# The last two token chunks of a fused attention and gated feed-forward kernel: first-layer blocks by seven half products, and a tail in a written step order

## The chip, the cores and the metric

The kernel runs on one core of a Trainium2 chip. A core has five engines with instruction queues of their own: TensorE (PE; its weight loads are shown as PEld), VectorE (DVE), ScalarE (ACT), GpSimd (POOL) and SyncE (SP, which here issues DMAs). Each takes its instructions in order, and semaphores tie them together. The metric is the device time of one execution in microseconds, the median of several runs.

## The reference, cut to what matters

The input is q, k and v of 8 batches, 8 heads, 576 positions and 64 values per head. Attention is computed twice, once on positions averaged by fours and once within a band of three neighbours, and the two are added. The result, 4608 tokens of 512 values, goes through a gated feed-forward layer:

```
x    = attention output, as (4608, 512)
gate = max(x @ w_gate, 0)        # w_gate 512 x 1536
val  = x @ w_val                 # w_val  512 x 1536
out  = (gate * val) @ w_out      # w_out 1536 x 512
```

The change is in this layer alone, in its last 1024 tokens.

## The kernel before, in words

Attention works on 32 head pairs. Its output lies transposed in xT: four blocks of 128 model values (index kk) by 4608 tokens, f16. The feed-forward layer works on nine chunks (0 to 8) of 512 tokens.

**First layer.** For a chunk c and a block jj of 128 of the 1536 ff values, `emit_h_mm` (line 585, its matmul at 588) makes the gate's half of the block by four matmuls (128x128 weights, 512 tokens, one for each kk) into one PSUM bank, and the value's half by four into the next. `emit_relu` (L605, ACT) writes max(gate, 0) as f16 into r1, and `emit_gate` (L609, DVE) multiplies r1 by the value's bank into gT[c % 2], block jj, f16. PSUM has eight banks of 512 f32 columns: `pair(i)` is banks 2i and 2i+1.

**Second layer.** A `Unit` (class at L655) makes 256 tokens (u = 0 or 1) of a chunk. It is already a two-by-two block product with seven products in place of eight: the 12 ff blocks are two halves of six, the 256 tokens two halves of 128, the 512 outputs two halves of 256. DVE forms four sums of gT blocks (s1 to s4, L678), the sums of w_out are made once (`emit_wt`, L651), and the steps p1 to p7 (`mm`, L684) are six matmuls of 256 columns each. Products p1, p6, p7 and p4 add up in one region a, and between them ACT copies a away (`keep`, L718) so that the partial sums can be used; p5 and p3 add up in b, p2 is alone in d. DVE adds d or b to a kept copy and writes the output tile (c11 at L721, c12 at L725, c22 at L733), ACT copies a itself (c21, L729). `emit_out` (L635) issues the output DMAs on SP.

**What sets the order.** The engines are scheduled by hand: instructions go into each queue in the order in which the Python code emits them. Chunks 2 to 6 follow a written order of steps, ORDER, in `emit_periods`; a step's mark `<` or `>` moves it to the chunk before or after. The last part, from the end of chunk 6's first layer, follows loops: `emit_tail_slot` for eight slots (chunks 7 and 8, three ff blocks each), each with half of the second-layer products of the chunk before, then the two units of chunk 8, `last`, one after the other in step order p1, p2, p6, p5, p7, p4, p3. In the first tail slot three gate matmuls and three value matmuls of chunk 7 are put ahead of product p2, into the banks of `pair(1)`.

The tail's units keep their sums in buffers that attention has left: `sa` in the tiles of v (shown as vw), `sums` in a q tile and two v tiles.

The softmax here doesn't subtract the row's maximum and nothing guards it: scores larger than these inputs give would overflow.

## Time and profile before

| | us |
|---|---|
| median of 8 runs | 350.72 |
| lowest and highest of them | 348.71, 351.86 |
| the profiled execution, its own time | 350.76 |
| its span, from first to last instruction | 348.9 |
| PE busy in the span | 340.2 |
| DVE, ACT, POOL busy | 274.8, 214.6, 190.7 |
| first product of unit (6,0), where the tail begins | 275.91 |
| start of the last DVE instruction | 345.69 |

Times within the span are counted from its start. A profile page has the busy time of each engine, the span in 40 slices of 8.7 us with a digit for the busy tenths of each, the DMA queues, the chain of work that ended last (followed back from the last instruction to whatever released each step), and the costliest groups of instructions. A group's line has the source line, the engine, the operation, the tiles written and read, shapes and count, then busy us and the mean ns of one, then the idle time ahead of them and who ended it. [...]

### The profile page before, as it was taken

To read this page: it belongs to the slowest core of one execution; us is meant where nothing else is said; L and a number is where in the kernel's file an instruction comes from. 1 tells how busy PE (TensorE), PEld (TensorE's weight loads), DVE (VectorE), ACT (ScalarE), POOL (GpSimd) and SP (SyncE) were. 2 spreads that over 40 slices of the span, in tenths; PEclk is the share of its full clock that TensorE was granted. 3 is DMA by queue.
4 is the path that set the end of the run, shared out by engine and by line. 5 is a ranking of instruction groups with operands and counts; after the bars stand their busy time and mean duration, and the time that the engine had idled before them with its cause. 6 is when DMAs were issued, how large, how long until landed. Compare 5 with 4: busy or idle time off the path is not lost. (4 is left out here: it accounts for less than half of the span.)

```text
span 348.9 us, 7968 instructions
## 1 busy us (share of the span) xinstructions
PE 340.2 (98%) x3127; PEld 205.3 (59%) x3127; DVE 274.8 (79%) x479; ACT 214.6 (61%) x390; POOL 190.7 (55%) x233
## 2 busy tenths in 40 slices
PE   7999999999999999999999999999999999999996
PEld 3665555545565756575656565665666555655575
DVE  4896656787899999999999999999989755354481
ACT  3657777587666776677667766676777433333332
POOL 8986556899999893979397959640300000000000
PEclk9999999999999999999999999999999999999999
DMA  9999999999999999999999998991101001001013
GB/s 147 166 171 186 185 191 159 155 155 188 176 152 162 168 185 73 136 147 185 79 127 161 156 98 89 151 154 25 61 3 60 2 30 46 31 32 45 18 45 120
DMA packets 168772, 40.29 MB, mean 115 GB/s; under 512 B 150080, under 2 KB 165664, under 8 KB 168736
## 3 DMA queue, kind: packets, MB, share of 16 engines
q0 software_dynamic: 132960, 22.93, 89.1%
q1 hardware_dynamic: 35056, 15.79, 24.6%
q10 hardware_dynamic: 720, 1.08, 1.0%
q8 instruction: 24, 0.39, 0.5%
q14 instruction: 12, 0.10, 0.1%
HBM read 46.45 MB, written 9.44 MB: 160 GB/s over the span
## 5 line engine op out<-in xcount | busy, mean ns | idle before, releaser
L588 PE MATMUL ps<-xT,wg_sb 128*128 128x512 f16 x432 | 110.0, 380 | 0.1
L588 PE MATMUL ps<-xT,wv_sb 128*128 128x512 f16 x432 | 109.6, 379 | 0.5 <-DVE gT L609 0.5
L609 DVE TENSOR_TENSOR gT<-r,ps 128x512 f16<-128x512 f16 x108 | 73.1, 683 | 38.3 <-PE ps L588 30.9
L605 ACT ACTIVATE r<-ps 128x512 f16<-128x512 f32 x108 | 64.2, 595 | 50.1 <-PE ps L588 48.4
L588 PEld LDWEIGHTS <-wv_sb 128*128 128x128 f16 x432 | 41.0, 98 | 47.0 <-issue 1.0
L588 PEld LDWEIGHTS <-wg_sb 128*128 128x128 f16 x432 | 39.9, 98 | 36.9 <-DVE xT L581 0.6
L545 DVE TENSOR_TENSOR xn<-ps,rden 64x720 f16<-64x720 f32 x46 | 41.7, 906 | 7.1 <-ACT rden L541 6.0
L376 ACT ACTIVATE ee<-ps 112x576 f16<-112x576 f32 x64 | 38.1, 648 | 10.9 <-PE ps L366 9.8
L536 ACT ACTIVATE rden<-ps 64x720 f32<-64x720 f32 x46 | 35.2, 765 | 14.8 <-PE ps L526 13.8
L233 POOL DMA_DIRECT2D qk<-in_q_dram x46 | 33.7, 735 | 6.8 <-DMA wo_sb<-in_moe_w_out_dram 2.8
L327 POOL TENSOR_TENSOR vd<-v 72x256 f16<-72x256 f32 x23 | 19.9, 874 | 29.6 <-PE ps L526 29.0
L233 POOL DMA_DIRECT2D qk<-in_k_dram x46 | 33.7, 735 | 1.3 <-DMA qkT<-qk 0.8
L684 PEld LDWEIGHTS <-gT 128*128 128x128 f16 x288 | 28.2, 98 | 10.3
L382 DVE TENSOR_TENSOR ee<-ee,cst_sb 112x576 f16<-112x576 f16 x64 | 30.4, 497 | 3.2 <-ACT ee L376 2.5
L258 POOL DMA_DIRECT2D vw<-in_v_dram x30 | 28.7, 957 | 6.9 <-PE ps L339 3.1
L321 POOL TENSOR_TENSOR v<-v 72x512 f32<-72x512 f16 x23 | 29.3, 1272 | 3.5 <-DMA v<-in_v_dram 2.9
L275 DVE TENSOR_REDUCE qkd<-qkT 128x288 f16<-128x1152 f16 x23 | 30.9, 1345 | 0.0
L718 ACT COPY q<-ps 128x256 f32<-128x256 f32 x39 | 14.5, 372 | 21.3 <-PE ps L684 20.9
L684 PEld LDWEIGHTS <-xo 128*128 128x128 f16 x240 | 22.6, 98 | 7.7 <-DVE xo L678 0.9
L684 PE MATMUL ps<-wo_sb,gT 128*128 128x256 f16 x192 | 24.9, 273 | 0.0
L504 DVE TENSOR_TENSOR xT<-xn 128x576 f16<-128x576 f16 x28 | 23.7, 846 | 0.6
L390 ACT ACTIVATE ed<-ps 72x576 f16<-72x576 f32 x32 | 20.6, 643 | 0.0
(103 smaller groups left out, 477.7 us busy)
## 6 DMA issues: line engine op xcount, KB each, us to landing
out_dram<-y_sb SPq DMA_DIRECT2D x20, 256.0 KB, 3.4
vw<-in_v_dram POOLq DMA_DIRECT2D x30, 168.0 KB, 6.7
qk<-in_q_dram POOLq DMA_DIRECT2D x46, 72.0 KB, 6.2
qk<-in_k_dram POOLq DMA_DIRECT2D x46, 72.0 KB, 6.5
v<-in_v_dram POOLq DMA_DIRECT2D x23, 144.0 KB, 6.2
out_dram<-y_sb SPq DMA_DIRECT2D x22, 128.0 KB, 1.7
wg_sb<-in_moe_w_gate_dram POOLq DMA_DIRECT2D x4, 384.0 KB, 9.9
wv_sb<-in_moe_w_val_dram POOLq DMA_DIRECT2D x4, 384.0 KB, 10.8
```

The costliest lines, as they stand in the source:

```text
L233: nc.gpsimd.dma_start(dst.rearrange("p (j h d) -> p j h d", h=2, d=64)[:, :, hh, :], _dap(src, off + hh * S * D, [[D, 96], [NQ * D, NB], [ ...
L258: nc.gpsimd.dma_start(t, _dap(v, base, [[D, WK], [NQ * D, n], [1, D]]))
L275: nc.vector.tensor_reduce(out=qkd[hp % 2].rearrange("p i t -> p (i t)"), in_=qkT[hp % 4][:, 0 : 2 * S].rearrange("p (t f) -> p t f", f=4), ...
L321: nc.gpsimd.tensor_tensor(out=m, in0=t[:, :, 0:128], in1=t[:, :, 128:256], op=ALU.add)
L376: nc.scalar.activation(out=o, in_=ps[0:WK, p0 + 2 * g : p0 + 2 * g + 2, 0:288], func=AF.Exp, scale=scale)
L382: nc.vector.tensor_tensor(out=o, in0=o, in1=_sap(masks_sb, (0, WK), 288 * g, [[0, 2], [1, 288]]), op=ALU.mult,)
L536: nc.scalar.activation(out=rden[lo : lo + 64], in_=ps[de : de + 64, 4 + 2 * hh : 6 + 2 * hh, 0:360], func=AF.Ln)
L545: nc.vector.tensor_tensor(out=xn[lo : lo + 64], in0=ps[lo : lo + 64, 4 + 2 * hh : 6 + 2 * hh, 0:360], in1=rden[lo : lo + 64], op=ALU.mult,)
L588: nc.tensor.matmul(out=pair(pp)[:, which, :], lhsT=w[:, kk, bass.ts(jj, 128)], rhs=xT[:, kk, c * TCH : (c + 1) * TCH], start=(kk == 0), st ...
L605: nc.scalar.activation(out=r1, in_=pair(pp)[:, 0, :], func=AF.Relu)
L609: nc.vector.tensor_tensor(out=gT[c % 2][:, jj, :], in0=r1, in1=pair(pp)[:, 1, :], op=ALU.mult)
L684: nc.tensor.matmul(out=out, lhsT=left[:, i, :], rhs=right[i], start=(first and i == 0), stop=(i == NK - 1), skip_group_check=True,)
```

## The change

In chunk 7 the gate's matrix for ff pairs j = 2 to 5, and in chunk 8 the gate's and the value's matrix for j = 0 to 5, are made by pairs (j, j+6) in the same seven-product form that the second layer has: the two ff blocks j and j+6 are one way to halve, the two halves of the 512 model values the other, and two halves of 256 tokens the third. A half product is two matmuls of 256 columns. The rest of chunk 7 (the gate for j = 0 and 1, all values) stays in four matmuls of 512 columns for each block.

For that, the sums of w_gate are made by DVE (`wg`, four of 128x1536) and those of w_val by POOL (`wv`, sixteen of 128x384); the differences of x (`xs`, four of 128x512 per chunk) by DVE. They lie in tiles that attention has left (ws in the q/k tiles and one v tile, xs, and the f32 result tiles ht in chunks of xT whose first layer is done, the kept copies hm in two v tiles). A `Block` has its three regions in two banks, as a unit of the second layer has: gate blocks in banks 0 and 1 or 2 and 3 by the parity of j, value blocks always in banks 4 and 5. `keep` copies partial sums by ACT, `out` writes the four quarters to ht: three by DVE adds, one by an ACT copy. The relu and the product with the value become one DVE instruction, with the value from PSUM (`gateg`) or from ht (`gateb`).

The loops of the tail give way to a written order, TAIL, of 424 steps, which every engine's queue follows. The four steps of ORDER that chunk 6 had left over (gate/4, gate/5, next/0, next/1) are in it. Units (6,u), (7,u) and (8,0) use banks 6 and 7, unit (8,1) banks 4 and 5, and the last chunk's sums are made in parts of three, two and one ff blocks (`part`). The order of the instructions ahead of the tail, and the 26 output DMAs' order on SP, are as before.

```diff
+TAIL = """
+wv/00/ p/1/60 gate/4 hg/0/71 wv/01/ gate/5 hg/0/70 wg/0/ hv/1/70 relu/0/70 sumhi/0/60 xs/0/7
+relu/0/71 hg/1/70 sumhi/1/60 wg/2/ hg/1/71 relu/1/70 wg/1/ keep/1/60 qg/1/72 qg/2/72 keepg/1/72
...
+qg/1/82 p/6/70 tv/11/81 gateb/0/80 qv/7/81 qg/4/81 keepv/3/81 qv/5/81 tg/22/81 p/3/61 keepg/1/82
...
+part/32/81 c22//81 p/3/80 c21//80 p/3/81 c12//80 p/4/81 c12//81 c21//81
+"""
-    def tail_unit(c, u, banks=(4, 5, 6)):
-        return Unit(c, u, [(k, 0) for k in banks], sa[u], sums[u], True)
+    def tail_unit(c, u):
+        k = 4 if (c, u) == (NCH - 1, 1) else 6
+        return Unit(c, u, ((k, 0), (k + 1, 0), (k + 1, 256)), sa[u], sums[u], True)
-    def emit_tail_slot(s, gate):
...
+    class Block:
+        def __init__(self, c, j, w, k):
+            self.c, self.j, self.w = c, j, w
+            self.a, self.b, self.d = (ps[:, b, lo : lo + 256] for b, lo in ((k, 0), (k + 1, 0), (k + 1, 256)))
+            self.t = ht[w][j % 2]
+            self.m = hm[w]
+        def q(self, i):
...
+            out, left, right = (
+                (self.a, g[:, 0:2, col], x_half(c, 0, 0)),
+                (self.d, g[:, 2:4, col], x_half(c, 1, 0)),
+                (self.b, s[3][:, :, col], x_half(c, 1, 1)),
+                (self.a, g[:, 2:4, bass.ts(j + NK, 128)], x[3]),
+                (self.b, s[0][:, :, col], x[0]),
+                (self.a, s[1][:, :, col], x[1]),
+                (self.a, s[2][:, :, col], x[2]),
+            )[i - 1]
+            for k in range(2):
+                nc.tensor.matmul(
+                    out=out,
+                    lhsT=left[:, k, :],
+                    rhs=right[:, k, :],
+                    start=(k == 0 and i in (1, 2, 5)),
+                    stop=(k == 1),
+                    skip_group_check=True,
+                )
+        def keep(self, i):
+            nc.scalar.copy(out=self.m[i], in_=self.a)
+        def out(self, arg):
...
+            if arg == "21":
+                nc.scalar.copy(out=o, in_=self.a)
+                return
+            src, m = {"11": (self.d, 0), "12": (self.b, 1), "22": (self.b, 2)}[arg]
+            nc.vector.tensor_tensor(out=o, in0=src, in1=self.m[m], op=ALU.add)
+    def block(c, j, w):
+        if (c, j, w) not in blocks:
+            blocks[c, j, w] = Block(c, j, w, 4 if w else 2 * (j % 2))
+        return blocks[c, j, w]
...
+        elif kind in ("gateg", "gateb"):
+            nc.vector.scalar_tensor_tensor(
+                out=gT[c % 2][:, j + NK * i, :],
+                in0=block(c, j, 0).t[i],
+                scalar=0.0,
+                in1=ps[:, 4 + i, :] if kind == "gateg" else block(c, j, 1).t[i],
+                op0=ALU.max,
+                op1=ALU.mult,
+            )
...
-        last = [tail_unit(NCH - 1, u, b) for u, b in ((0, (4, 5, 6)), (1, (7, 2, 3)))]
-        gate = lambda: None
-        for s in range(NP - LEAD, NCH * 4):
-            gate = emit_tail_slot(s, gate)
-        gate()
-        for x in last:
-            x.step("p1")
-        for which in (range(2), range(2, 4)):
-            for x in last:
-                x.sums(4, NK, which)
-        for p in ("p2", "p6", "p5", "p7", "p4", "p3"):
-            for x in last:
-                x.step(p)
+        for tok in TAIL.split():
+            kind, arg, *at = tok.split("/")
+            if at:
+                emit_tail_step(kind, arg, at[0])
+            else:
+                emit_step(kind, arg, 1, NCH - 3)
```

A step is read as kind/argument/place: `qg/6/84` is half product 6 of the gate for chunk 8, pair j = 4; `keepv/1/82` the first kept copy of the value for chunk 8, j = 2; `tg/22/83` the quarter 22 of the gate; `p/1/71` product 1 of unit (7,1).

## The prediction

> **What bounds the kernel now.** I read the page's shares first, then its forty slices, then the chain of work that ended last, and only then the groups of the last stage. On the page:

> ```profile
> PE 340.2 (98%) x3127; PEld 205.3 (59%) x3127; DVE 274.8 (79%) x479; ACT 214.6 (61%) x390; POOL 190.7 (55%) x233
> ...
> PE   7999999999999999999999999999999999999996
> ...
> DVE  4896656787899999999999999999989755354481
> ```

> PE is full from the second slice to the last. DVE is as full until slice 31 (about 270 us) and about half busy after it. The change lies in that last part, so what counts is who ends last there. The chain of waits, in order of time:

> ```profile
> 277.18 0.61 DVE gT L609
> 277.79 0.04 issue
> 277.83 0.81 PE ps L588 x3
> ...
> 334.74 1.73 PE ps L588 x8
> 336.47 9.20 PE ps L684 x84
> 345.67 0.02 issue
> 345.69 0.42 DVE y_sb L725
> ```

> From 277.83 on the chain is PE alone: no stall, first-layer groups of eight (L588) and products (L684) in turn. It also gives the prices: 8 matmuls of 512 columns in 1.73 us are **0.216 us each**, 84 of 256 columns in 9.20 us are **0.1095 us each**. So a matmul costs its columns, and half a matmul half the time. Before 277.83 PE stood still, the waits say 0.5 us "PE ps L588 <- DVE gT L609": the one stall of this stage. Busy time by stretch (sum, then PE, PEld, DVE, ACT, POOL):

> ```profile
> 277.00:290.00 13.00, 12.55 (x77) 7.37 (x76) 7.12 (x16) 4.24 (x9) 0.00 (x0) 1.00 0.09 32
> 290.00:310.00 20.00, 20.00 (x121) 11.69 (x120) 10.73 (x21) 6.64 (x13) 0.00 (x0) 1.00 0.10 34
> 310.00:330.00 20.00, 20.00 (x124) 11.95 (x122) 8.79 (x17) 6.64 (x13) 0.00 (x0) 1.00 0.09 33
> 336.50:345.70 9.20, 9.16 (x84) 7.93 (x82) 4.61 (x16) 2.98 (x8) 0.00 (x0) 1.00 0.21 71
> ```

> DVE has about half of its time free, ACT two thirds, POOL all; the granted clock is 1.00.

> **PE, the sum.** The tail starts at 275.91 with the first product of unit (6,0). Sixteen matrix-pairs (gate in ten, value in six) leave the plain form: each was 2 x 4 matmuls of 512 columns, 8 x 0.216 = 1.73 us, and becomes 7 half products of 2 matmuls of 256 columns, 14 x 0.1094 = 1.53 us. In all 128 x 0.2158 = 27.62 us go and 224 x 0.1094 = 24.51 us come: **3.11 us less**. The 64 other first-layer matmuls and the 252 of the units stay. The last stretch of before, 84 matmuls of 256 columns in a row, shows that weight loads keep up at this size (PEld 7.93 of 9.20 us). The stall of 0.45 us also goes: its wait (three value matmuls put behind the gate that frees their bank) is not in the new order. If it stayed, 0.45 us come back.

> **What comes for it on the others.** Per matrix-pair: three ACT copies that keep partial sums and one that evacuates, and three DVE adds into f32 tiles; the relus of these pairs go, and the gate becomes one scalar_tensor_tensor (max, then mult) per ff block: eight with one f32 SBUF source and one PSUM source, twelve with two f32 SBUF sources. DVE also gets four differences per chunk of tokens (512 elements) and four gate-weight sums (1536 elements); POOL sixteen value-weight sums of 384 elements. The rows, from the groups of the tail by form (the column before the last bar is busy us and mean ns):

> ```profile
> L609 DVE TENSOR_TENSOR gT<-r,ps 128x512 f16<-128x512 f16 x26 | 17.8, 686 | 26.3 <-PE ps L588 26.1
> L678 DVE TENSOR_TENSOR vw<-gT 128x768 f16<-128x768 f16 x7 | 3.9, 552 | 0.0
> L721 DVE TENSOR_TENSOR y_sb<-ps,v 128x256 f32<-128x256 f32 x3 | 1.3, 417 | 0.0
> ```

> and from the groups of the whole run:

> ```profile
> L545 DVE TENSOR_TENSOR xn<-ps,rden 64x720 f16<-64x720 f32 x46 | 41.7, 906 | 7.1 <-ACT rden L541 6.0
> ...
> L678 DVE TENSOR_TENSOR xo<-gT 128x768 f16<-128x768 f16 x15 | 9.4, 624 | 0.0
> ```

> Durations overlap when nothing is waited for. Two DVE lines of the timeline's end (start, duration):

> ```profile
> 339.18 0.42 DVE L721 TENSOR_TENSOR y_sb<-ps,q 128x256 f32<-128x256 f32 x1
> 339.52 0.41 DVE L721 TENSOR_TENSOR y_sb<-ps,v 128x256 f32<-128x256 f32 x1
> ```

> 0.42 us long, 0.34 us apart: an instruction on DVE occupies it for its duration less 0.08 us. In the same way the ACT copy (0.372 us) occupies 0.26.

> **The one unknown price** is the scalar_tensor_tensor: before has none. Its 512 elements cost 0.42 us at least, as the f16 SBUF difference of that size does (L678, 128x512), and 1.22 us at most, if two operations on f32 mean two passes (0.15 + 2 x 512 x 1.04 ns). Between: L609 takes 0.686, and L545, with an f32 source, 906 ns for 720 elements, which is 0.15 us + 1.05 ns per element and 0.69 us for 512. I take **0.69**: both rows with f32 operands move an element in about 1.04 ns, and the page shows no two-pass operation.

> [...]

> **Does DVE keep up?** Sums over the written order, in net times (0.336 an add of 256, 0.60 a gate, 0.468 a sum of 768, 0.87 a weight sum):
> - Stage one, to the last gate of chunk 7: PE 64 x 0.216 + 121 x 0.1094 = 27.05 us. DVE 16 adds 5.4, 6 plain gates 3.6, 8 new gates 4.8, weight sums 3.5, token differences 2.7, unit sums 3.9: 23.9 us. ACT 8.6.
> - Stage two, the six pairs of chunk 8: PE 269 x 0.1094 = 29.4 us. DVE 43 adds 14.4, unit sums 4.5, 12 new gates 7.3: **26.3 us**. ACT 54 copies, 14.4.
> - Stage three, units (8,0) and (8,1): PE 86 x 0.1094 = 9.4 us, DVE 6.4.

> DVE goes from half full to 89% in stage two, yet stays below PE in each. Averages hide waits, so I also laid these durations along the order, each instruction after its predecessor and its releasers. The hand-overs: 0.05 us from DVE to PE (277.79 to 277.83), 0.20 from the end of PE's last matmul slot to its reader (345.67 is the modelled end, the slot ends at 345.49, and DVE starts at 345.69), 0.03 from ACT to DVE. A keep then costs its own chain 0.20 + 0.37 + 0.05 = 0.62 us, and the order puts other half products there. PE's waits add up to **0.13 us**, none above 0.05. Behind a late DVE stand the third product on a bank and the next pair's first, and behind those everything on PE, so a late DVE shows at once.

> **Costed at nothing.** ACT (35 us of work in 66). POOL's sixteen sums: its last work of before ends at 248.2, they want about 15 us by the rate of L321's sums (1.27 us for 512 elements), and the first product that needs them is past 300 us; without that cover PE would wait for them whole. They share the chip with DVE between 248 and 270: L678 takes 0.62 us on average where POOL works and 0.55 where it rests, so the dozen SBUF sums and masks there gain up to 0.08 us each, 1 us in all, with 1.5 us of DVE idle beside it; between 120 and 200 us POOL is busy 63 of 80 us and PE never waits.

> [...]

> SP: its 26 output DMAs stand in the old order, and the last is issued 0.6 us after PE's last slot, as before (345.50 to 346.14).

> **Sum**, against the profiled execution (350.76 us, span 348.9; the median of the eight is 350.72, so the same): 350.76 - 3.11 - 0.45 + 0.13 = **347.3 us**.

> **Rivals.**
> 1. *DVE binds in part.* For: 89% in stage two. If a two-source gate costs 0.9 to 1.0 us, stage two's DVE is 28.8 to 30.0 us against 29.4, and along the order the waits grow by 0.7 to 1.8 us: 348.0 to 349.1. Against: both f32 rows.
> 2. *Slower: the new gate runs at half rate*, both forms at 1.22 us. DVE then has 28.2 against PE's 27.05 in stage one and 32.7 against 29.4 in stage two: by sums 4.4 us, along the order 7.1 us of waits, so 351.5 to 354.3. It decides from about 1.05 us per gate: there the waits eat the 3.56 us. If only the twelve are slow, the waits are 3.2 to 4.6 us and it ends at 350.4 to 351.8.
> 3. *The half products don't cost half.* Twenty-six weight loads wait for a semaphore, eleven did; a load that can't run ahead exposes 0.11 us, 2.9 us if all do: 350.2, no change. Against: nearly all of these releases are long past in the written order. A hand-over from ACT to PE of 0.2 us in place of 0.05 would cost 2 us, 349.3.

> **Chances.** The forecast 0.68, with its own range 346.5 to 348.1; rival 1: 0.12; rival 2: 0.12; rival 3: 0.08. This kernel's measurement tells about 0.3% (1.05 us) from no change. Faster than that: 0.68 + 0.09 + 0.03 = 0.80; within: 0.08; slower: 0.12. The range takes in rivals 1 and 3 and leaves out rival 2: 346.4 to 350.2.

> **What would show it.** Right: the chain stays PE through the tail with 540 matmuls; the new gates' mean is near 0.69 us; DVE near 26 us of net work in about 29.5 us of stage two. Wrong: waits "PE <- DVE" of microseconds behind the new gates (rivals 1, 2), or small ones "PE <- ACT" and idle weight loads (rival 3). A price of the new gates above 1 us would overturn the forecast.

## The result: slower by 1.5%, lost ahead of the tail

| | before | after |
|---|---|---|
| median of the runs, us | 350.65 (32 runs) | 355.27 (11 runs, 354.66 to 357.46) |
| profiled execution, its own time | 350.76 | 353.86 |
| its span | 348.9 | 351.8 |
| start of the tail (first product of unit (6,0)) | 275.91 | 282.49 |
| tail, to the start of the last matmul | 69.47 | 65.79 |

The ratio of the medians is 1.0145, with an interval of 1.0117 to 1.0173. The forecast was 347.3 us, faster, with a range up to 350.2: the sign is wrong and the range misses by 5 us.

The table already splits the error. The tail, the part that was rewritten, became 3.68 us shorter, nearly what the sum asked for (3.11 + 0.45 - 0.13 = 3.43 us). What is lost is lost before the tail begins, in attention, where none of attention's instructions was changed or moved. By the medians 4.62 us were lost in all, so about 8.3 us there (4.62 + 3.68).

The page of the changed kernel, shares and slices (8.8 us each; compare PE and POOL around slices 29 and 30, 246 to 264 us):

```profile
PE 337.1 (96%) x3223; PEld 214.8 (61%) x3223; DVE 306.9 (87%) x547; ACT 223.4 (64%) x434; POOL 205.3 (58%) x249
...
PE   6999999999999999999999999999659999999996
...
POOL 8986556989989995979396969703950000000000
PEclk9999999999999999999999999999969999999999
```

PE has a hole at 246 to 264 us that it had not before, the granted clock falls in the same place, and POOL works there. The chain of waits, in order of time, names the instruction:

```profile
247.64 0.90 DVE xn L587
248.54 0.33 DVE y_sb L767
248.87 8.54 DVE xT L546
257.42 0.47 DVE xo L720
257.88 0.37 DVE ee L424
...
260.51 2.48 PE ps L630 x8
...
338.07 10.49 PE ps L726 x96
```

L546 is attention's SBUF sum of 576 f16 elements (L504 in before), which takes 0.74 us. Here one of its 28 takes 8.6 us. The timeline of the same stretch (start, duration) shows what ran beside it:

```profile
245.64 0.73 POOL L369 TENSOR_TENSOR vd<-v 72x256 f16<-72x256 f32 x1
...
246.34 6.13 POOL L902 TENSOR_TENSOR qk<-wv_sb 128x384 f16<-128x384 f16 x7
...
248.79 8.62 DVE L546 TENSOR_TENSOR xT<-xn 128x576 f16<-128x576 f16 x1
...
252.42 3.52 POOL L902 TENSOR_TENSOR qk<-qk,wv_sb 128x384 f16<-128x384 f16 x4
255.89 0.91 POOL L902 TENSOR_TENSOR qk<-wv_sb 128x384 f16<-128x384 f16 x1
...
258.40 0.40 PE L560 MATMUL ps<-ee,vw 112*128 112x96 f16 x3 [6.08 <-DVE ee L424]
```

POOL's line L902 is the value-weight sums, the `wv` steps. They are written among the steps of the tail, but their operands lie ready and POOL has nothing else to wait for, so they start as soon as POOL's last work for attention (L369) is done, 36 us before the tail. Twelve come back to back, from 246.34 to 256.80. DVE's sum starts among them at 248.79 and ends 0.6 us after the last of them. Behind it on DVE stands the mask of `ee` (L424), for which PE waits 6.1 us. The view by source line shows that this is one long instance and not a slower row (ns: min, median, max):

```profile
L546 DVE TENSOR_TENSOR xT<-xn x28: 741/758/8620, 36.7 to 282.3; 128x576 f16<-128x576 f16 x28
```

And the granted clock (columns: sum; busy us of PE, PEld, DVE, ACT, POOL with counts; clock; DMA share; GB/s):

```profile
250.00:255.00 5.00, 2.32 (x11) 0.88 (x9) 5.00 (x1) 1.79 (x4) 5.00 (x6) 1.00 0.08 32
255.00:258.00 3.00, 0.00 (x0) 0.00 (x0) 3.00 (x3) 0.00 (x0) 1.80 (x3) 0.51 0.00 0
258.00:262.00 4.00, 3.25 (x25) 2.10 (x26) 3.08 (x5) 2.06 (x3) 1.91 (x3) 0.51 0.01 4
262.00:266.00 4.00, 3.87 (x29) 2.57 (x29) 3.70 (x5) 1.87 (x5) 1.61 (x2) 1.00 0.00 0
```

PE is idle from 252.3 on; at about 255.1 the clock falls to half and stays there until 261.9, though PE works again from 258.4. Of these last 3.5 us PE waits 0.35 and works at 0.50 of the clock for the rest, so by estimate the clock costs about 1.6 us more. PE's waits of 6.4 us in this stretch (6.1 and 0.35) and these 1.6 us make 8.0 us. From the DVE instruction ahead (L545 at 248.50, L587 at 246.71) to the tail's start the two profiles differ by 8.4 us (27.41 against 35.78), so 0.4 us are not traced to a wait. The 1.8 us by which the changed kernel's profiled execution is early at that point lie in earlier, unchanged code.

### The profile page after: what moved, and what is told of

Its sections match the earlier page's. It is cut to its first block, busy times and chain, and to the rows that moved or that the text cites. A ratio compares the mean times of both kernels' runs of the same rounds, so it can differ in the third digit from the quotient of the medians.

```text
span 351.8 us, 8307 instructions
## 1 busy us (share of the span) xinstructions
PE 337.1 (96%) x3223; PEld 214.8 (61%) x3223; DVE 306.9 (87%) x547; ACT 223.4 (64%) x434; POOL 205.3 (58%) x249
## 4 chain that ended last, share of the span: by engine, by line
PE 86%; DVE 10%; DMA 2%; ACT 1%; issue 1%; POOLq 0%
PE ps L630 43%; PE ps L726 19%; PE ps L936 7%; PE ps L560 3%; PE ps L660 3%; DVE xT L546 3%; PE ps L397 2%; PE ps L408 2%; PE ps L336 2%; PE ps L568 2%; DVE xn L587 2%; DMA qk<-in_k_dram 2%; DVE xo L720 1%; DVE gT L651 1%; DVE xo L482 1%; DVE ee L424 1%
## 5 line engine op out<-in xcount | busy, mean ns | idle before, releaser
L630 PE MATMUL ps<-xT,wv_sb 128*128 128x512 f16 x384 | 97.9, 381 | 0.0
L630 PE MATMUL ps<-xT,wg_sb 128*128 128x512 f16 x352 | 89.0, 380 | 0.1
L651 DVE TENSOR_TENSOR gT<-r,ps 128x512 f16<-128x512 f16 x88 | 59.3, 681 | 12.0 <-ACT r L647 6.3
L647 ACT ACTIVATE r<-ps 128x512 f16<-128x512 f32 x88 | 52.2, 594 | 27.6 <-PE ps L630 27.3
L630 PEld LDWEIGHTS <-wv_sb 128*128 128x128 f16 x384 | 36.5, 98 | 38.9 <-issue 1.1
L630 PEld LDWEIGHTS <-wg_sb 128*128 128x128 f16 x352 | 32.0, 98 | 32.3 <-DVE xT L623 0.6
L587 DVE TENSOR_TENSOR xn<-ps,rden 64x720 f16<-64x720 f32 x46 | 41.7, 905 | 5.1 <-ACT rden L583 4.0
L369 POOL TENSOR_TENSOR vd<-v 72x256 f16<-72x256 f32 x23 | 20.3, 893 | 27.4 <-PE ps L568 26.8
L424 DVE TENSOR_TENSOR ee<-ee,cst_sb 112x576 f16<-112x576 f16 x64 | 32.0, 523 | 2.5 <-ACT ee L418 1.8
L726 PEld LDWEIGHTS <-gT 128*128 128x128 f16 x288 | 28.2, 98 | 7.7
L546 DVE TENSOR_TENSOR xT<-xn 128x576 f16<-128x576 f16 x28 | 30.9, 1104 | 0.6
L363 POOL TENSOR_TENSOR v<-v 72x512 f32<-72x512 f16 x23 | 29.6, 1286 | 2.7 <-DMA v<-in_v_dram 2.2
L560 PE MATMUL ps<-ee,vw 112*128 112x96 f16 x276 | 21.1, 208 | 7.2 <-DVE ee L424 7.1
L946 ACT COPY vw<-ps 128x256 f32<-128x256 f32 x48 | 16.6, 374 | 16.1 <-PE ps L936 10.8
```

The source lines that it names most:

```text
L424: nc.vector.tensor_tensor(out=o, in0=o, in1=_sap(masks_sb, (0, WK), 288 * g, [[0, 2], [1, 288]]), op=ALU.mult,)
L546: nc.vector.tensor_tensor(out=xT[:, kk, b * S : (b + 1) * S].rearrange("p (c t f) -> p c t f", c=2, f=4), in0=x[:, :, 0:288].rearrange("p ...
L560: nc.tensor.matmul(out=ps[:, bank, NQ * j : NQ * j + NQ], lhsT=vflat[:, v0 : v0 + 128], rhs=e[:, hh, lo : lo + NQ], start=True, stop=True,)
L587: nc.vector.tensor_tensor(out=xn[lo : lo + 64], in0=ps[lo : lo + 64, 4 + 2 * hh : 6 + 2 * hh, 0:360], in1=rden[lo : lo + 64], op=ALU.mult,)
L630: nc.tensor.matmul(out=pair(pp)[:, which, :] if out is None else out, lhsT=w[:, kk, bass.ts(jj, 128)], rhs=xT[:, kk, c * TCH : (c + 1) * TCH],
L647: nc.scalar.activation(out=r1, in_=pair(pp)[:, 0, :] if h1 is None else h1, func=AF.Relu)
```

## The experiments

The theory: POOL's back-to-back weight sums hold DVE's sum, and that costs all that was lost; the tail does what was forecast. Rivals: the tail's new work costs something too; or something else moved attention. Kernels of one batch stand against runs of the kernel before on the same chip, whose median is given in brackets.

### Without POOL's sums

```diff
-            x, s = xs[c - NCH + 2], ws[self.w]
+            x, s = xs[c - NCH + 2], ws[0]
...
-            emit_ws(1, i, 192 * int(arg[1]), 192 * int(arg[1]) + 192, nc.gpsimd)
+            pass
```

> The changed kernel without POOL's sixteen weight sums; the value's half products 3, 5, 6 and 7 read the gate's weight sums in their place, so the value of chunk 8 is wrong. Theory (POOL's sums, run back to back from 246 us, hold up DVE's 576-element sum at L546 for 8 us): that sum is back to 0.75 us and the kernel takes 347.3 us, as forecast, since the tail itself ran in 65.95 us against 66.0 forecast. Rival A (the time is lost in the tail, by its many DVE and ACT hand-overs): still near 355. Rival B (a 6 us stall comes from elsewhere in attention, and POOL only happens to be busy then): 353 to 355.

Measured: 346.79 us [350.10], ratio 0.9909 (0.9876 to 0.9942); tail 65.79 us, and from 246 to 275 us PE is busy the whole time at clock 1.00. Against its own before that is 3.31 us less, where the forecast had 3.43: without the sums, the rest of the sum holds, and nothing else moved attention.

### The sums alone, in the kernel before

After `emit_periods`, before gets the same sixteen sums into the same tiles, and nothing reads them:

```diff
+        for tok in "00 01 20 21 02 03 22 10 11 12 13 23 30 31 32 33".split():
+            i, lo = int(tok[0]), 192 * int(tok[1])
...
+            nc.gpsimd.tensor_tensor(out=o, in0=x, in1=y, op=op)
```

> The kernel before, with the sixteen weight sums added to POOL at the end of the written order; nobody reads them. Theory: DVE's next sum of two SBUF sources behind about 248 us waits 7 to 8 us, PE stands still for 6 us and then runs some us at a reduced granted clock: 350.7 + 7 to 8.5 = 358 to 359 us. Rival A and B: 350.7, the tail is the old one.

Measured: 359.37 us [350.10], ratio 1.0285 (1.023 to 1.034). The timeline has the same picture, with nothing of the new tail in the kernel:

```profile
250.38 8.60 DVE L504 TENSOR_TENSOR xT<-xn 128x576 f16<-128x576 f16 x1
```

PE's wait for the mask behind it is 6.1 us again, the tail is before's 69.47 us, and the clock is 0.50 from 258.5 to 265.3. The sums alone cost 9.3 us here (by the interval 8 to 12). The cause is shown from both sides: taking them out gives the forecast, putting them in gives the loss.

### The sums on DVE

```diff
-            emit_ws(1, i, 192 * int(arg[1]), 192 * int(arg[1]) + 192, nc.gpsimd)
+            emit_ws(1, i, 192 * int(arg[1]), 192 * int(arg[1]) + 192, nc.vector)
```

"Lock" in the expectation stands for a DVE sum that is held up by POOL's sums.

> The changed kernel with the sixteen sums on DVE, at the same steps of the written order. Theory: no lock; DVE gets 16 x (0.35 - 0.08) = 4.3 us more in stages one and two, where it had 23.9 of 27.05 and 26.3 of 29.4 us; laid along the order PE's waits grow from 0.13 to 0.83 us: 348.0 us, faster than before. Rival A: DVE is the tail's limit, so all 4.3 us come on top of 355: 357 or more. Rival B: 353 to 355.

Measured: 347.58 us [350.10], ratio 0.9931 (0.9903 to 0.9959); the tail 66.60 us. DVE takes the sixteen sums at the same steps for 0.8 us of the tail. With the sums on DVE the change is worth having.

### The sums on POOL, one at a time

A difference of 128x2 on POOL ahead of each sum reads what DVE's latest gate, token difference or gate-weight sum before it has written (`seen`), so that each sum starts where it is written:

```diff
+    seen = [xT[:, NPB - 1, NTOK - 2 : NTOK]]
...
+            seen.append(gT[c % 2][:, j + NK * i, 0:2])
...
+            k = 2 * (4 * i + int(arg[1]))
+            nc.gpsimd.tensor_tensor(out=zero_sb[:, k : k + 2], in0=seen[-1], in1=seen[-1], op=ALU.subtract)
             emit_ws(1, i, 192 * int(arg[1]), 192 * int(arg[1]) + 192, nc.gpsimd)
```

> The changed kernel with the sums still on POOL, each behind a two-element POOL difference that reads what DVE's latest step of the written order wrote, so that the sums spread over the tail's first 27 us and leave gaps. Theory: no long block; each sum can hold a DVE instruction of two SBUF sources by at most 0.92 us, and stage one has 3 us of DVE to spare, so 347.3 to 349.5 us. [...] Rivals A and B: 353 to 355.

Measured: 348.16 us [350.10], ratio 0.9954 (0.9924 to 0.9985); the tail 67.62 us. Here no DVE sum with two SBUF sources is held for more than 0.77 us, less than one POOL sum (0.9 us). This one is 128 elements long and takes about 0.22 us alone:

```profile
277.95 0.94 DVE L720 TENSOR_TENSOR vw<-gT 128x128 f16<-128x128 f16 x1
```

So even sums apart from one another cost 1.8 us of the tail, more than the same sums on DVE itself (0.8 us).

### How long is the hold: half of the sums

Before, with the first eight sums of the list only.

> The kernel before with the first eight of the sixteen sums on POOL; nobody reads them. If a run of POOL sums without a gap holds DVE until it ends (theory 1): POOL works from 248 to 255.1, the 576-element DVE sum that starts near 250.4 ends near 255.7 in place of 251.1, 4.6 us late; PE stands still for about 3 us, and the granted clock falls for less time than after 6 us or not at all: 353.5 to 355.5 us. If each POOL sum holds a DVE instruction for its own remainder at most (theory 2), none over 0.9 us: 350.5 to 352.

Measured: 355.22 us [349.54], ratio 1.0135 (1.007 to 1.0201). POOL's run is from 248.74 to 255.73, and DVE's sum ends 0.6 us after it:

```profile
251.20 5.14 DVE L504 TENSOR_TENSOR xT<-xn 128x576 f16<-128x576 f16 x1
```

The hold follows the run's length, not the DVE instruction's. PE's longest wait is 2.6 us here (254.7 to 257.3), and yet the clock falls, after PE is back at work:

```profile
257.50:258.00 0.50, 0.19 (x5) 0.09 (x3) 0.50 (x2) 0.00 (x0) 0.00 (x0) 1.00 0.00 0
258.10:261.40 3.30, 3.19 (x21) 1.80 (x21) 2.06 (x4) 2.52 (x4) 0.00 (x0) 0.50 0.02 5
261.50:265.00 3.50, 3.50 (x28) 2.28 (x27) 3.44 (x6) 1.12 (x3) 0.00 (x0) 1.00 0.00 0
```

### The same sums with gaps

Before, with all sixteen, each followed by a POOL instruction that only writes (0.63 us):

```diff
             nc.gpsimd.tensor_tensor(out=o, in0=x, in1=y, op=op)
+            nc.gpsimd.memset(zero_sb, 0.0)
```

> The kernel before with all sixteen sums on POOL, each followed by a POOL memset of 128x640 zeros, which reads no SBUF; nobody reads the sums. Theory 1 (DVE is let in when the run of POOL sums has a gap): no DVE instruction is longer than about 1.7 us, a dozen of them wait up to 0.9 us each, DVE has 1.5 us to spare, so 351 to 356 us and no fall of the clock. Theory 3 (any POOL work holds DVE off, whatever it reads): one block of 12 x 1.6 us, about 19 us: 368 us or more.

Measured: 351.00 us [349.54], ratio 1.0025 (0.9988 to 1.0062). DVE's sum waits, but gets in between two of POOL's:

```profile
249.56 1.93 DVE L504 TENSOR_TENSOR xT<-xn 128x576 f16<-128x576 f16 x1
```

The same amount of POOL work costs nothing that can be told from zero once it has gaps, and the clock stays at 0.999. At this place it is the unbroken run that does the harm.

### A version that beats both

The sums on DVE in eight pieces of twice the width, and at other steps of the written order: three of the four pieces that the last ff pairs need go into stage two (the new TAIL is not shown).

```diff
...
+    W = 384
...
-            emit_ws(1, i, 192 * int(arg[1]), 192 * int(arg[1]) + 192, nc.gpsimd)
+            emit_ws(1, i, W * int(arg[1]), W * int(arg[1]) + W, nc.vector)
```

> The changed kernel with the value's weight sums on DVE, in eight pieces of 768 elements in place of sixteen of 384, and moved in the written order to where DVE has time (the second halves into stage two, ahead of ff pair 3). DVE's added net work is 8 x 0.47 = 3.7 us; laid along the order PE's waits are 0.13 us, as little as forecast for the change itself: 347.3 us against 350.7, 0.5 us below the version with the sums at their old steps. If DVE at 95% lets waits through that the sums of durations don't show: 348 to 349.

Measured: **346.08 us** (345.75 to 346.61) [349.54], ratio 0.9882 (0.9828 to 0.9936), the lowest of all, though the interval overlaps those of the kernel without the sums and of the one with sixteen on DVE. PE waits for nobody from 240 us on, and the tail is 65.79 us, as if the sums were free. One of its windows, over stage two:

```profile
303.00:330.00 27.00, 27.00 (x249) 24.08 (x248) 26.43 (x66) 16.78 (x51) 0.00 (x0) 1.00 0.13 46
```

DVE is busy for 26.43 of 27 us and PE is still full. Little room is left there for another DVE instruction.

### Why one sum is held through the whole run

All that follows asks why one DVE sum was held over a whole run. First, the changed kernel with the run behind attention's end: one POOL difference ahead of the first sum reads attention's last output.

```diff
+            if arg == "00":
+                last_x = xT[:, NPB - 1, NTOK - 2 : NTOK]
+                nc.gpsimd.tensor_tensor(out=zero_sb[:, 0:2], in0=last_x, in1=last_x, op=ALU.subtract)
```

> The changed kernel with the sums on POOL behind one wait, for attention's last output, and then back to back: the same place as the paced version, without its gaps. Theory 1: the run of 14 us from about 276 holds the first DVE sum of two SBUF sources (the gate's weight sum) until near 290, DVE has 3 us to spare in stage one, PE stands still for some 9 us and its clock falls: 357 to 361 us. Theory 2: as the paced version, 348 to 350.

Measured: 352.44 us (one execution); the tail 72.89 us. The theory that a run of sums holds DVE until it ends (theory 1) fails here: the two take turns. The timeline's DVE sum, 0.95 us alone, and POOL's seven sums, 6.13 us when they ran through:

```profile
274.74 7.73 POOL L902 TENSOR_TENSOR qk<-wv_sb 128x384 f16<-128x384 f16 x7
...
280.03 1.68 DVE L902 TENSOR_TENSOR qk<-wg_sb 128x1536 f16<-128x1536 f16 x1
```

No DVE sum is held for more than 0.73 us, each of POOL's may wait for one of DVE's, and in the tail so many short holds make DVE late: PE waits 3.8 us for a token difference (L911, `xs`) and 1.6 us for an add (L955), and the clock is 0.50 from 284.0 to 287.4. Late, the sums cost 7.1 us of tail (72.89 - 65.79) in another way.

Then, before, with the sixteen sums behind the output of the very DVE sum that was held:

```diff
+        seen = xT[:, 0, 8 * S - 2 : 8 * S]
+        nc.gpsimd.tensor_tensor(out=zero_sb[:, 0:2], in0=seen, in1=seen, op=ALU.subtract)
```

> The kernel before with the sixteen sums on POOL without gaps, behind a two-element POOL difference that reads what the 576-element DVE sum at 250.6 us (L504) wrote; nobody reads the sums. So the run starts just after that sum, at about 251.4, and meets f16 sums and masks of plain rows first. Theory F (only a form like L504's, with a source that repeats each element four times, is held for the whole run; plain rows alternate with POOL, as in the late version): no DVE instruction before the next L504 at 264.3 is over 1.7 us, 351 to 354 us. Theory 1 (a run without gaps holds any DVE instruction of two SBUF sources until it ends, where the run starts first): one of 9 to 10 us, 357 to 360 us.

Measured: 351.00 us [350.33], ratio 1.0008 (0.9968 to 1.0049): turns again, and no DVE instruction beyond 1.5 us. (The profiled execution was the longest of the ten, 354.98 us, so only the order of events is taken from it.)

```profile
255.01 6.88 POOL L1038 TENSOR_TENSOR qk<-wv_sb 128x384 f16<-128x384 f16 x7
...
255.15 1.08 DVE L382 TENSOR_TENSOR ee<-ee,cst_sb 112x576 f16<-112x576 f16 x1 [0.16 <-ACT ee L376]
```

Is it the form of the held instruction? The late kernel again, with one more DVE sum of exactly L546's form put beside POOL's run:

> The late version (sums on POOL without gaps behind attention's last output, 352.4 us) with one more DVE sum behind the first gate-weight sum: 576 elements of L504's form, its second source repeating each element four times; nobody reads it. Theory F: it is held until the run of POOL sums ends, 8 us or more, and the time is 359 to 364 us. If the form makes no difference: under 1.7 us and 352 to 354.5 us.

Measured: 355.54 us (one execution). The added sum:

```profile
279.83 1.46 DVE L989 TENSOR_TENSOR xo<-xn 128x576 f16<-128x576 f16 x1
```

It is held for 0.7 us, no more: the form (theory F) doesn't decide. Nor does a form with two f32 SBUF sources:

> The late version with one more DVE sum behind the first gate-weight sum: 576 elements in plain rows, two f32 SBUF sources, f16 out; nobody reads it. It goes at one element per 1.04 ns, as L504 does, but without the repeated source. If the rate is what lets POOL hold it (theory F, by rate): 8 us or more, 359 to 364 us. If the repeated source is (theory F, by pattern) or nothing of the form: under 1.7 us and 352 to 354.5 us.

Measured: 358.07 us (one execution, in which attention had already taken some us longer before the tail began, so its time says little); the added sum took 1.47 us, where the one of L546's form took 1.46.

Is it the small instruction that waits at the head of the runs that took turns? Before with the sixteen sums and a 128x2 difference at the head that waits for nothing:

> The kernel before with the sixteen sums on POOL at the place where they held a DVE sum for 8.6 us (359.4 us), and one two-element POOL difference ahead of them that has nothing to wait for; nobody reads any of it. If that small instruction at the head is what lets DVE alternate with POOL in the other versions (theory D1): no DVE instruction over 1.7 us, 350.5 to 353 us. If it makes no difference: 8.6 us again and 358 to 361 us.

Measured: 357.50 us (one execution) [348.84], and the hold is back in full:

```profile
248.43 8.76 DVE L504 TENSOR_TENSOR xT<-xn 128x576 f16<-128x576 f16 x1
```

A small instruction that waits for nothing (D1) doesn't decide.

Is it that the run was already under way, with only PSUM reads on DVE, when the sum came? Before with the sums behind a DVE sum's output (at 256.5 us in before's profile), a place where the run is 2 us old when DVE's next two-SBUF-source instruction arrives:

> The kernel before with the sixteen sums behind a two-element POOL difference that reads what the DVE sum at 256.5 us (L678) wrote; nobody reads any of it. The run then starts near 257.2 and is 2 us old, with only PSUM-reading DVE instructions beside it, when the next DVE sum of two SBUF sources comes at 259.4. [...] If the held place in attention is special to its own instruction (D2), or the small one at the head decides (D1): alternation, 350.5 to 353 us.

Measured: 350.63 us (one execution) [348.84]; turns again, and the next DVE sum of two SBUF sources, 2.2 us into the run, takes 1.22 us (0.55 alone):

```profile
254.76 0.19 POOL L1025 TENSOR_TENSOR zero_sb<-xo 128x2 f16<-128x2 f16 x1 [8.95 <-DVE xo L678]
254.91 7.66 POOL L1038 TENSOR_TENSOR qk<-wv_sb 128x384 f16<-128x384 f16 x7
...
257.07 1.22 DVE L678 TENSOR_TENSOR xo<-gT 128x768 f16<-128x768 f16 x1
```

The run's age falls too. **What stays open**: in the four kernels with the full hold (the changed one, all sums in before, half of them, and those with the small instruction at the head) POOL goes from its last attention sums (L321 and L327; L363 and L369 in the changed kernel) into the run without a stop. In the five whose run took turns (late, late with either added sum, behind the held sum, later run) POOL had stood idle just before. That fits all nine, but no kernel changed that alone, so it is a pattern and not shown as a cause. In all five, POOL was idle because it waited for a DVE instruction, so the idle time and that wait can't be told apart. And the place itself (D2 in the last expectation) is not excluded: in all four long holds it is the same instruction of attention that is held, and in none of the five did a run without gaps meet that one.

## Why the prediction was wrong, step by step

- **PE's sum, 3.11 us less, and the stall of 0.45 us: right.** The tail is 65.79 us where before's was 69.47. PE waits for nobody in the tail; its chain from 300 us to 348.57 us is PE alone.
- **The new gate at 0.69 us: right.** The groups of the tail:

```profile
L976 DVE SCALAR_TENSOR_TENSOR gT<-xT 128x512 f16<-128x512 f32 x12 | 7.9, 685 | 0.1
L976 DVE SCALAR_TENSOR_TENSOR gT<-xT,ps 128x512 f16<-128x512 f32 x8 | 5.4, 681 | 0.2 <-PE ps L630 0.2
```

Two f32 SBUF sources cost no more than one from PSUM (685 against 681 ns), and rivals 1 and 2, which wanted 0.9 us or more, did not happen.
- **Weight loads and hand-overs: right.** 96 matmuls of 256 columns take 10.49 us in the last stretch, 0.1093 each; rival 3 did not happen either.
- **DVE keeps up: right.** Stage two's windows of after, of which two:

```profile
310.00:320.00 10.00, 10.00 (x94) 8.96 (x92) 9.44 (x24) 5.82 (x18) 0.00 (x0) 1.00 0.16 55
320.00:330.00 10.00, 10.00 (x94) 8.96 (x93) 9.15 (x23) 6.63 (x20) 0.00 (x0) 1.00 0.15 54
```

Full PE beside a DVE that is over nine tenths busy.
- **"Costed at nothing", POOL's sixteen sums beside DVE between 248 and 270 us: wrong, and this is the whole error.** The step priced the sharing by a mean, 0.62 against 0.55 us of L678, "up to 0.08 us each, 1 us in all", hidden by 1.5 us of idle time. One instruction alone came 7.9 us late (8.62 against 0.74 us), and the stretch lost 8.4 us. Two things failed. First, the mean was taken over sums that mostly met nobody. Before's trace has the other end, in the view by source line (ns: min, median, max) and in the timeline:

```profile
L504 DVE TENSOR_TENSOR xT<-xn x28: 741/758/1598, 37.7 to 275.7; 128x576 f16<-128x576 f16 x28
...
88.93 1.49 POOL L233 DMA_DIRECT2D qk<-in_q_dram  x2
89.14 1.60 DVE L504 TENSOR_TENSOR xT<-xn 128x576 f16<-128x576 f16 x1
...
203.29 1.17 POOL L321 TENSOR_TENSOR v<-v 72x512 f32<-72x512 f16 x1
203.73 1.36 DVE L504 TENSOR_TENSOR xT<-xn 128x576 f16<-128x576 f16 x1
...
209.37 1.46 POOL L321 TENSOR_TENSOR v<-v 72x512 f32<-72x512 f16 x1
209.75 1.50 DVE L678 TENSOR_TENSOR xo<-gT,xo 128x768 f16<-128x768 f16 x1
```

The longest instance, 1.60 us, runs beside DMA issues of POOL and not beside a sum. Of the seven instances of L504 that overlap a POOL sum, four took 1.03 to 1.36 us and three 0.74; L678 took up to 1.50 us where 0.55 is usual. So a meeting cost up to 0.95 us (1.50 against 0.55), beside a POOL sum of 1.46. Second, POOL's work between 120 and 200 us was taken as the model (busy 63 of 80 us). But that is mostly the issuing of DMAs; the sums are L321 and L327, 19.5 us, and there never more than two in a row:

```profile
L233 POOL DMA_DIRECT2D qk<-in_q_dram x20 | 14.6, 736 | 1.0 <-DMA qk<-in_k_dram 0.4 <-DMA v<-in_v_dram 0.4
L233 POOL DMA_DIRECT2D qk<-in_k_dram x18 | 13.3, 743 | 0.8 <-DMA qkT<-qk 0.8
L321 POOL TENSOR_TENSOR v<-v 72x512 f32<-72x512 f16 x9 | 11.2, 1246 | 0.2
L327 POOL TENSOR_TENSOR vd<-v 72x256 f16<-72x256 f32 x9 | 8.3, 934 | 11.3 <-PE ps L526 11.2
```

The new ones come as twelve in a row, 10.5 us, and one DVE instruction was held through all that was left of them. The idle time beside it was no cover, since close behind it in DVE's queue was a mask that PE needs.

The sum with two SBUF sources was held, and the reads from PSUM beside the same run were not (L587, 0.91 us at 246.71 and 0.90 at 247.64 beside POOL's sums, 0.906 before). In the runs that took turns a hold was 0.73 us at most, less than one POOL sum (0.91 us). The long hold goes further: one instruction was held through all the sums that were left in the row, some nine.

- **What the prediction didn't have at all**: with PE's wait of 6.1 us (252.3 to 258.4) came a granted clock of 0.50, from 255.1 to 261.9. Of the 8.4 us, about 1.6 by estimate are this clock after the wait.
- **Chances.** Every rival was about the tail, where the change is written; none had its place in attention, where its first instructions run. POOL's sums beside DVE were named, with their stretch, costed at nothing, and given no chance of their own.

## What to carry to other kernels

An instruction without a wait runs when its engine is free, not where it is written (here 36 us ahead of the tail that it is written in): see what its queue is doing then, and whom it can hold up there. For two engines that hold each other up, read the longest instances of a row and what they met, not the mean, and ask how many instructions come in a row; then cost the wait by what stands behind the held instruction in its queue. In this kernel POOL's sums cost 9.3 us in an unbroken run and nothing that can be told from zero with gaps between them; on DVE itself, eight pieces placed with care cost nothing of the tail and made the version with the lowest time, 346.08 us.

- A DVE sum with two SBUF sources (0.74 us) was held for 8.6 us by twelve POOL sums in a row and for 5.1 us by eight, until 0.6 us after the run's end; with 0.63 us of a write-only POOL instruction between the sums the longest was 1.93 us. In five kernels where POOL had been idle ahead of the run, DVE and POOL took turns, and a DVE sum lost at most 0.73 us. Why is open.
- In these runs the granted clock didn't fall at a fixed time after PE fell idle. In the changed kernel it fell to 0.50 after 2.7 us (252.3 to 255.1), with the sums alone in before after 4.6 us (253.9 to 258.5), and with eight sums at 258.1, when PE had been idle for only 2.6 us and back at work for 0.7. It stayed at 0.50 for 6.8, 6.8 and 3.4 us; in the changed kernel it came back 3.5 us after PE worked again (258.4 to 261.9).
- A scalar_tensor_tensor on 512 elements takes 0.685 us with two f32 SBUF sources and 0.681 us with one in PSUM: no more than a plain product of that size (0.686).
